# One conversion slot, one load and one buffer offset moved in an attention and feed-forward kernel

## The chip, the cores and the metric

The kernel runs on one core of a Trainium2 chip. Its metric is the device time of one execution in microseconds, and the time of a version is the median of several runs. In the profiles PE is the matrix engine (PEld is its loading of weights), DVE the vector engine, ACT the scalar engine, POOL the general engine, and SP the engine that issues most of the DMAs.

## The reference

```
scores = q @ k.T / sqrt(64) + bias        # 4 batches, 8 heads, 576 x 576; the bias is a small MLP
                                          # of log1p(|i-j|) / log1p(max(i,1)), 8 heads, no batch
attn   = softmax(scores) @ v              # float32
x      = attn, heads side by side         # 2304 tokens x 512
h      = x @ w_in                         # 512 x 2048
out    = (h * tanh(softplus(h))) @ w_out  # 2048 x 512
```

The two weight matrices come in as 64-bit floats, and the kernel itself turns them into 32-bit ones.

## The kernel before

**Three stages.** The bias stage makes the 36 row tiles of the bias, copies each from PSUM to an SBUF tile `bt` (`evac`, lines 500 to 514) and writes it to DRAM. The `bt` tiles take turns in eight buffers. The attention stage follows, and takes over the SBUF memory of the bias stage as soon as the DMAs that read it are done: its tiles `main` and `tail` (lines 266 to 300) lie where `bt` lay. The feed-forward stage comes last. The first three steps of the attention stage run inside the bias stage already.

**A pair and its steps.** The attention stage works on 16 pairs, 0 to 15, each one batch and two heads, in five steps n = 5 i + x of one block of query rows each, in the order 0, 1, 4, 2, 3. The text calls x = 0 to 4 the first to the fifth step. In a step `scores` puts the score matmuls on PE (line 220), `add_bias` lets DVE add the bias and take the row minimum, one instruction for each head (line 237), `exps` lets ACT take the exponentials (line 252), `transposes` turns the tiles of two steps before on PE (lines 287, 290), ACT copies these out of PSUM (lines 295 to 300), and `pv_duo` multiplies with v on PE (lines 313, 317). DVE copies the result out at line 320, which in the fourth step comes behind that step's conversion slots. Block 4 in the third step has half as many rows, so ACT has one exponential there and not two. The scores of a step use both PSUM buffers, so the scores of the next step can't start before `add_bias` has read them.

**Everything is in program order.** Each engine takes its instructions in the order in which the code gives them, so what waits holds back all that is behind it on that engine.

**q and k.** From pair 3 on the scores are three products of a rounded part `hi` and a rest `lo`. `load_qk` of pair i + 1 is called in the first step of pair i: SP loads the raw values into `rawqk` (one buffer, line 166), POOL loads the same values rounded into `qkhi` (two buffers, line 167), and POOL then takes four differences for `qklo` (line 170). Behind the raw load SP has v (line 176) and whatever the step has besides.

**Conversion slots.** `split` spends a number of slots per step on the weights. A job of 512 columns takes four: a multiplication (line 118 on DVE, or line 116 on ACT when its slot falls in the third step), a shift (line 121), and two combining instructions on DVE (lines 123 and 125). Line 123 reads what the multiplication wrote. Line 125 ends the job and issues the load of the next but one (line 104), into the buffer that it has just left. Nine slots fall in a pair, so the phase of the jobs comes round every four pairs. For the first four jobs ACT (line 135) and POOL (line 136) also split the result into two parts.

Of the kernel before, what the change touches and what calls it, by code (L numbers as in the profile page):

```python
# [7 lines left out]
F32 = mybir.dt.float32  # L8
# [7 lines left out]
B, H, S, D, C = 4, 8, 576, 64, 32  # L16
# [3 lines left out]
P = 128  # L20
SH = S // 2
KO = 640
QW = KO + S
# [21 lines left out]
def kernel(ctx: ExitStack, tc, qk, v, wb, w2, w_in, w_out, psia, psi4, rinv, eye, out):  # L45
    nc = tc.nc
    pe, dve, act, pool, sp = nc.tensor, nc.vector, nc.scalar, nc.gpsimd, nc.sync
# [48 lines left out]
    def load_weights():  # L96
        while todo and len(w64) < 2:
            kind, g, k = job = todo.pop(0)
            w = convp.tile([P, 512, 2], U32, name="w64")
            if kind == "i":  # L100
                src = w_in[k * P:(k + 1) * P, g * 512:(g + 1) * 512]
            else:
                src = w_out[(4 * g + k) * P:(4 * g + k + 1) * P, :]
            sp.dma_start(out=w.rearrange("p f t -> p (f t)"), in_=src.bitcast(U32))
            w64.append((job, w))

    def conv_weights(on_act):

        job, w = w64.pop(0)
        late = order.index(job) >= EARLY
        c = (ring if late else convp).tile([P, 512], F32, name="w32")
        cu = c.bitcast(U32)
        if on_act:
            act.mul(c, w.bitcast(F32)[:, :, 1], 2.0 ** -112)
        else:
            dve.tensor_scalar(c, w.bitcast(F32)[:, :, 1], 2.0 ** -112, None, op0=ALU.mult)

        def parts():  # L120
            dve.tensor_scalar(w[:, :, 0], w[:, :, 0], 29, None, op0=ALU.logical_shift_right)
            yield False
            dve.scalar_tensor_tensor(cu, cu, 3, w[:, :, 0], op0=ALU.logical_shift_left, op1=ALU.bitwise_or)  # L123
            yield False
            dve.scalar_tensor_tensor(cu, w[:, :, 1], 0x80000000, cu, op0=ALU.bitwise_and, op1=ALU.bitwise_or)  # L125
            w32.append((job, c))
            yield True
        return parts()

    def split_weights(eng):  # L130
        job, c = w32.pop(0)
        if job not in w_hi:
            w_hi[job] = ring.tile([P, 512], F32R, name="wh{}{}{}".format(*job))
            w_lo[job] = ring.tile([P, 512], F32R, name="wl{}{}{}".format(*job))
        act.copy(w_hi[job], c)
        eng.tensor_tensor(w_lo[job], c, w_hi[job].bitcast(F32), op=ALU.subtract)
# [12 lines left out]
    hip = rsbuf("hip", 2, side="right")  # L149
    biasp = rsbuf("biasp", side="right")  # L150
    s_ps = rpsum("s_ps", 2, side="right")
    qk_t, v_t, bias_t = {}, {}, {}
    PLAIN = 3
    st.tile([P, 32], F32, name="fill", bufs=1)
    x0 = lsbuf("x0")

    def load_qk(i):
        hp, b = divmod(i, B)
        if i < PLAIN:
            qk_t[i] = [rawp.tile([P, 1280], F32, name="qklo")] * 2  # L160
            sp.dma_start(out=qk_t[i][0][:, :QW], in_=qk[b, hp])
            return
        raw = hip.tile([P, 1280], F32, name="rawqk", bufs=1)
        hi = hip.tile([P, 1280], F32R, name="qkhi")
        lo = rawp.tile([P, 1280], F32R, name="qklo")
        sp.dma_start(out=raw[:, :QW], in_=qk[b, hp])
        pool.dma_start(out=hi[:, :QW], in_=qk[b, hp])
        for c0 in (608, 912, 0, 304):
            sl = slice(c0, c0 + 304)
            pool.tensor_tensor(lo[:, sl], raw[:, sl], hi[:, sl].bitcast(F32), op=ALU.subtract)  # L170
        qk_t[i] = hi, lo

    def load_v(i):
        hp, b = divmod(i, B)
        vt = vp.tile([P, 2, 5, D], F32, name="vt")
        sp.dma_start(out=vt, in_=v[b, hp].rearrange("p (h c d) -> p h c d", h=2, c=5))
        v_t[i] = vt

    def load_raw(i):
        load_qk(i)  # L180
        load_v(i)
# [3 lines left out]
    def load_bias(hp, c):  # L185
        h0, h1 = 2 * hp, 2 * hp + 1
        rows = P if c < 4 else 64
        src = bias_d[c][:, :rows * PITCH].rearrange("h (i j) -> h i j", j=PITCH)[:, :, PAD:PAD + S]
        if c < 3 and hp % 2 == 0:
            pool_, name = ((xa, "xhi"), (xa, "xlo"), (x0, "xraw"))[c]  # L190
            t = pool_.tile([P, HP * TB], F32, name=name)[:, :2 * S]
        else:
            t = biasp.tile([P, 2 * S if c < 4 else S], F32, name=f"bias{c}")
        bias_t[hp, c] = t
        if c < 4:
            sp.dma_start(out=t[:, 0:S], in_=src[h0])
            sp.dma_start(out=t[:, S + 64:], in_=src[h1, :, 0:512])
            sp.dma_start(out=t[:, S:S + 64], in_=src[h1, :, 512:S])
        else:
            sp.dma_start(out=t[TOP], in_=src[h0])  # L200
            sp.dma_start(out=t[LOW, 64:], in_=src[h1, :, 0:512])
            sp.dma_start(out=t[LOW, 0:64], in_=src[h1, :, 512:S])

    NPAIR = B * HP
# [129 lines left out]
    def load_x(blk, p):  # L334
        t0, n = blocks[blk]
        raw = p.tile([P, HP, TB], F32, name="xraw", bufs=1)
        for off, m, b, s in _x_runs(t0, n):
            sp.dma_start(out=raw[:, :, off:off + m], in_=x_d[b][:, :, s:s + m])
        x_raw[blk] = raw

    def load_r(blk, r, h0, h1):

        t0, n = blocks[blk]
        for off, m, b, s in _x_runs(t0, n):
            while m:
                k = min(m, 512 - s) if s < 512 else m
                for u in range(2):
                    if s < 512:
                        src = r_d[b][h0:h1, 4 * u:4 * u + 4].rearrange("p c j -> p (c j)")[:, s:s + k]
                    else:  # L350
                        src = r_d[b][h0:h1, 8, 64 * u + s - 512:64 * u + s - 512 + k]
                    sp.dma_start(out=r[64 * u:64 * u + 64, :, off:off + k],
                                 in_=src.unsqueeze(0).to_broadcast([64, h1 - h0, k]))
                off, m, s = off + k, m - k, s + k

    def ahead(n):

        i, x = divmod(n, 5)
        if x == 0 and i + 1 < NPAIR:
            load_raw(i + 1)  # L360
        c = {(1, 3): 0, (2, 1): 1, (2, 3): 2, (3, 2): 4, (3, 4): 3}.get((i % B, x))
        if c is not None and i // B + 1 < HP:
            load_bias(i // B + 1, c)
        if n == NS - 11:
            load_x(0, x0)
        if n == NS - 10:
            x_hi[0] = xa.tile([P, HP, TB], F32R, name="xhi")
            x_lo[0] = xa.tile([P, HP, TB], F32R, name="xlo")
            load_r(0, x_lo[0].bitcast(F32), 0, HP)
        if NS - 5 <= n < NS - 1:  # L370
            d = n - (NS - 5)
            x, hi, lo = (y[0][:, d] for y in (x_raw, x_hi, x_lo))
            dve.tensor_tensor(hi, x, lo.bitcast(F32), op=ALU.mult)
            pool.tensor_tensor(x, x, lo.bitcast(F32), op=ALU.mult)
            pool.tensor_tensor(lo, x, hi.bitcast(F32), op=ALU.subtract)

    def split(n):

        i, x = divmod(n, 5)
        for _ in range(((2, 1, 2, 2, 2) if n > 25 else (2, 1, 3, 2, 2) if n > 4 else (0,) * 5)[x]):  # L380
            if not conv and w64:
                conv.append(conv_weights(x == 2))
            elif conv and next(conv[0]):
                conv.clear()
                load_weights()
                if w32[0][0] in order[:EARLY]:
                    split_weights(pool)
# [55 lines left out]
    bo = bsbuf("bo", 8)  # L443
# [19 lines left out]
    NW = S + 15  # L463

    def reach(t):

        left, right = 16 * t + 15, S - 16 * t
        n = max(left + 1, right)
        return left, right, n + n % 2
# [6 lines left out]
    for idx, t in enumerate(ts):  # L476
        spent["a"] += 1.0 + (1.9 if idx in SOFT_AT else 0.0)
        spent["v"] += (1.7 if idx in SOFT_AT else 0.0)
        n = reach(t)[2]
# [6 lines left out]
    def make_h(idx):  # L486
        if idx >= NB:
            return
        n = reach(ts[idx])[2]
        for cg in range(4):  # L490
            e = maker[idx, cg]
            ht = ring.tile([P, 640], F32, name="ht")
            k = 4 * ts[idx] + cg
            if e == "a":
                act.activation(ht[:, :n], at[:, :n], AF.Relu, bias=bb[:, k:k + 1])
            else:
                dve.tensor_scalar(ht[:, :n], at[:, :n], bb[:, k:k + 1], 0.0, op0=ALU.add, op1=ALU.max)
            h_t[idx, cg] = ht

    def evac(idx):  # L500
# [12 lines left out]
        dst = bias_d[c][:, a:a + 16 * (PITCH + 1)].rearrange("h (i j) -> i h j", j=PITCH + 1)  # L513
        sp.dma_start(out=dst[:, :, :NW], in_=bt)

    make_h(0)
    make_h(1)
    sp.dma_start(out=ident, in_=eye)
    for idx in range(NB + 2):
        if idx < NB:  # L520
            t = ts[idx]
            make_h(idx + 2)
            n = reach(t)[2]
# [218 lines left out]
```

## Time and profile before

| | us |
|---|---|
| three runs, median (lowest to highest) | 702.86 (701.67 to 703.18) |
| the profiled execution's own time | 702.7 |
| its span in the trace | 700.9 |
| of the span, attention steps from the first pair on | 66 to 299 |
| of the span, feed-forward stage | 299 to 700 |

The profiled execution's own time is 1.8 us longer than its span, and 0.2 us under the median of the runs. A timeline row gives the start, the duration, the engine, the line of the kernel and the tiles, and in brackets the engine's idle time before it with what ended that. Neighbouring instructions of one line are merged, and a row of such a merge ends in the number of its instructions.

### The profile page before, as it was taken

The numbers are of one execution on the slowest core, as the hardware profiler recorded it, in microseconds if no ns is written. First come the engines' busy times: TensorE is split into PE (matmuls) and PEld (weight loads), VectorE is DVE, ScalarE is ACT, GpSimd is POOL, SyncE is SP. The second block draws the span as 40 slices with busy tenths as digits, with TensorE's granted clock in tenths as the row PEclk, the third lists the DMA queues.
The fourth block names the chain that finished last, engine by engine and source line by source line (L and its number), as shares of the span: only waits on it lengthen the run. The fifth ranks groups of instructions, "written<-read, shape, count | busy, mean of one in ns | idle before, by whom it ended". The sixth has DMA issues, their size and how long they took to land.

```text
span 700.9 us, 13630 instructions
## 1 busy us (share of the span) xinstructions
PE 672.9 (96%) x5156; PEld 511.2 (73%) x5156; DVE 517.3 (74%) x1082; ACT 458.4 (65%) x987; POOL 72.4 (10%) x85
## 2 busy tenths in 40 slices
PE   5878999999999999999999999999999999999997
PEld 2224666776777666668888888889988888888886
DVE  7995898888988878868788566655775567665554
ACT  6895988888899888876675544444554455454443
POOL 0000142322222222710000000000000000000000
PEclk9999999999999999999999999999999999999999
DMA  4997688787778767204000120023005000010001
GB/s 150 318 285 228 195 273 263 216 284 225 245 234 266 241 231 240 55 22 116 1 1 0 66 56 1 1 76 106 1 1 150 1 1 0 1 60 1 1 0 60
DMA packets 46081, 81.88 MB, mean 117 GB/s; under 512 B 14400, under 2 KB 23104, under 8 KB 46016
## 3 DMA queue, kind: packets, MB, share of 16 engines
q1 hardware_dynamic: 43568, 72.70, 32.8%
q0 software_dynamic: 1872, 8.09, 3.9%
q8 instruction: 40, 0.66, 0.4%
q10 hardware_dynamic: 576, 0.22, 0.1%
q14 instruction: 25, 0.20, 0.1%
HBM read 60.60 MB, written 20.40 MB: 116 GB/s over the span
## 4 chain that ended last, share of the span: by engine, by line
PE 71%; ACT 9%; DVE 7%; DMA 3%; issue 2%; DVEq 0%; ACTq 0%
PE h L589 28%; PE y L627 28%; PE o L313 5%; PE s L220 5%; ACT pt L252 5%; DVE pt L237 4%; ACT main L295 3%; PE tp L287 3%; PE tp L290 1%; DMA w<-in_w_in_dram 1%; DMA w<-in_w_out_dram 1%; PE o L317 1%; DVE w L123 1%; DVE x L320 1%; DVE w L125 1%
## 5 line engine op out<-in xcount | busy, mean ns | idle before, releaser
L252 ACT ACTIVATE pt<-pt,m 128x576 f32<-128x576 f32 x144 | 112.2, 780 | 33.5 <-DVE m L237 32.9
L627 PE MATMUL y<-who,ghi 128*128 128x512 f32 x288 | 112.1, 389 | 0.0
L627 PE MATMUL y<-wlo,ghi 128*128 128x512 f32 x288 | 112.1, 389 | 0.0
L627 PE MATMUL y<-who,glo 128*128 128x512 f32 x288 | 112.0, 389 | 0.0
L611 ACT CAST ghi<-e 128x512 fp32r<-128x512 f32 x72 | 44.7, 621 | 93.5 <-DVE e L607 93.5
L237 DVE CUSTOM_DVE_ANT_0 pt<-s,bias 128x576 f32<-128x576 f32 (+1 forms) x112 | 81.3, 753 | 17.8 <-PE s L220 16.6
L594 ACT ACTIVATE e<-h 128x512 f32<-128x512 f32 x72 | 43.0, 597 | 65.9 <-PE h L589 65.7
L595 DVE TENSOR_SCALAR e<-e 128x512 f32<-128x512 f32 x72 | 30.6, 426 | 74.0 <-ACT e L594 74.0
L612 DVE TENSOR_TENSOR glo<-e,ghi 128x512 fp32r<-128x512 f32 x72 | 49.8, 692 | 44.9 <-ACT ghi L611 44.9
L589 PE MATMUL h<-xhi,whi 128*128 128x512 f32 (+1 forms) x320 | 79.1, 369 | 0.0
L589 PE MATMUL h<-xhi,wli 128*128 128x512 f32 (+1 forms) x320 | 78.7, 368 | 0.0
L589 PE MATMUL h<-xlo,whi 128*128 128x512 f32 (+1 forms) x320 | 78.7, 368 | 0.0
L313 PE MATMUL o<-main,vt 128*64 128x320 f32 (+1 forms) x512 | 73.8, 411 | 3.1 <-DVE x L320 3.0
L295 ACT COPY main<-tp 128x512 f32<-128x512 f32 x126 | 66.5, 577 | 2.0 <-DMA bias_d<-bt 1.9
L287 PE MATMUL tp<-ident,pt 64*128 64x64 f32 x1184 | 61.7, 227 | 6.3 <-ACT main L295 4.7
L589 PEld LDWEIGHTS h<-xhi,whi 128*128 128x128 f32 x320 | 57.1, 188 | 11.7 <-issue 0.7
L287 PEld LDWEIGHTS tp<-ident,pt 64*128 64x128 f32 x1184 | 53.5, 139 | 15.2 <-ACT main L295 13.1
L589 PEld LDWEIGHTS h<-xhi,wli 128*128 128x128 f32 x320 | 56.9, 189 | 10.0
L589 PEld LDWEIGHTS h<-xlo,whi 128*128 128x128 f32 x320 | 56.9, 189 | 10.0
L627 PEld LDWEIGHTS y<-who,glo 128*128 128x128 f32 x288 | 54.1, 188 | 11.3
L627 PEld LDWEIGHTS y<-who,ghi 128*128 128x128 f32 x288 | 54.1, 188 | 11.0
L627 PEld LDWEIGHTS y<-wlo,ghi 128*128 128x128 f32 x288 | 54.1, 188 | 10.9
(69 smaller groups left out, 1126.9 us busy)
## 6 DMA issues: line engine op xcount, KB each, us to landing
bias_d<-bt SPq DMA_DIRECT2D x36, 295.5 KB
w<-in_w_in_dram SPq DMA_DIRECT2D x16, 512.0 KB
w<-in_w_out_dram SPq DMA_DIRECT2D x16, 512.0 KB
qkhi<-in_qk_dram POOLq DMA_DIRECT2D x13, 608.0 KB, 4.5
rawqk<-in_qk_dram SPq DMA_DIRECT2D x13, 608.0 KB
vt<-in_v_dram SPq DMA_DIRECT2D x16, 320.0 KB
out_dram<-w SPq DMA_DIRECT2D x17, 256.0 KB
x_d<-x SPq DMA_DIRECT2D x32, 128.0 KB
```

What stands on the lines that cost most here:

```text
L220: pe.matmul(s[:, j, :SH], q[rows, c * P:(c + 1) * P], k[rows, KO + j * SH:KO + (j + 1) * SH], start=(t == 0), stop=(t == len(terms) - 1))
L237: dve.tensor_tensor_reduce(out=halves(pt[rows, sl]), in0=s[rows, :, :SH], in1=halves(bt[rows, sl]), scale=-0.125, scalar=BIG, op0=ALU.add, ...
L252: act.activation(ps, ps, AF.Exp, bias=m[:, u:u + 1], scale=-1.0, accum_out=sums[i][:, k:k + 1])
L287: pe.transpose(tp[:, k * 64:k * 64 + 64], pt[rows, c0:c0 + P], ident[rows, rows])
L295: copy(main[:, :, :, q0:q0 + 64], tp.rearrange("p (h k q) -> p h k q", h=2, k=4))
L313: pe.matmul(o[h * 64:h * 64 + 64, :w], vt[:, h, k, :], main[:, h, k, :], start=(k == 0), stop=False, **kw)
L589: pe.matmul(h[:, u * n:(u + 1) * n], w["i", g4, d][:, r * P:(r + 1) * P], x[:, d, :n], start=(k == 0), stop=(k == 11))
L594: act.activation(e, h, AF.Exp)
L595: dve.tensor_scalar(e, e, E20, None, op0=ALU.min)
L611: act.copy(ghi, e)
L612: dve.tensor_tensor(glo, e, ghi.bitcast(F32), op=ALU.subtract)
L627: pe.matmul(ys[blk][t], g[:, c0:c0 + P], w, start=(f == 0 and k == 0), stop=(f == NFC - 1 and k == 2))
```

## The change

Three things are moved. The conversion slots per step go from (2, 1, 2, 2, 2) to (2, 1, 3, 1, 2) after step 25, and from (2, 1, 3, 2, 2) to (2, 2, 3, 1, 2) in steps 5 to 25. The raw load of a pair is issued in the fourth step of the pair but one before it, two steps sooner than it was; the rounded load and the differences on POOL stay where they were in the code. And four `bt` tiles that nothing uses are taken ahead of the bias stage's first one, so that each row tile uses the buffer that is four further on in the turn.

```diff
+    def load_plain(i):
+        hp, b = divmod(i, B)
+        qk_raw[i] = hip.tile([P, 1280], F32, name="rawqk", bufs=1)
+        sp.dma_start(out=qk_raw[i][:, :QW], in_=qk[b, hp])
...
-        raw = hip.tile([P, 1280], F32, name="rawqk", bufs=1)
+        raw = qk_raw.pop(i)
         hi = hip.tile([P, 1280], F32R, name="qkhi")
         lo = rawp.tile([P, 1280], F32R, name="qklo")
-        sp.dma_start(out=raw[:, :QW], in_=qk[b, hp])
         pool.dma_start(out=hi[:, :QW], in_=qk[b, hp])
...
         if x == 0 and i + 1 < NPAIR:
             load_raw(i + 1)
+        if x == 3 and PLAIN <= i + 2 < NPAIR:
+            load_plain(i + 2)
...
-        for _ in range(((2, 1, 2, 2, 2) if n > 25 else (2, 1, 3, 2, 2) if n > 4 else (0,) * 5)[x]):
+        for _ in range(((2, 1, 3, 1, 2) if n > 25 else (2, 2, 3, 1, 2) if n > 4 else (0,) * 5)[x]):
...
+    for _ in range(4):
+        bo.tile([P, NW], F32, name="bt")
     make_h(0)
     make_h(1)
```

## Rows read from the trace of the kernel before

**Rows 1.** The page, busy time, share of the span and instructions of each engine.
```profile
PE 672.9 (96%) x5156; PEld 511.2 (73%) x5156; DVE 517.3 (74%) x1082; ACT 458.4 (65%) x987; POOL 72.4 (10%) x85
```

**Rows 2.** Windows over the attention steps: busy us (instructions) by engine, PE clock, DMA.
```profile
66.00:299.00 233.00, 226.04 (x2816) 160.81 (x2813) 199.29 (x499) 200.44 (x523) 68.89 (x77) 1.00 0.71 226
```

**Rows 3.** Timeline of pair 10, third to fifth step: start us, us, engine, line.
```profile
215.33 0.70 ACT L116 ACTIVATE w<-w 128x512 f32<-128x512 f32 x1
...
215.72 0.76 DVE L237 CUSTOM_DVE_ANT_0 pt<-s,xraw 128x576 f32<-128x576 f32 x1 [1.84 <-PE s L220]
...
217.09 0.71 DVE L123 SCALAR_TENSOR_TENSOR w<-w,w 128x512 uint32<-128x512 uint32 x1
...
217.83 0.69 DVE L125 SCALAR_TENSOR_TENSOR w<-w,w 128x512 uint32<-128x512 uint32 x1
...
218.32 0.29 PE L220 MATMUL s<-qkhi,qklo 64*128 64x288 f32 x2
...
218.44 0.48 DVE L320 COPY x<-o 128x320 f32<-128x320 f32 x1
...
218.84 0.75 DVE L237 CUSTOM_DVE_ANT_0 pt<-s,bias 128x576 f32<-128x576 f32 x1
...
219.69 0.78 ACT L252 ACTIVATE pt<-pt,m 128x576 f32<-128x576 f32 x1 [0.35 <-DVE m L237]
```

**Rows 4.** Timeline of pair 12, second to fifth step.
```profile
241.29 0.36 SPq L166 DMA_DIRECT2D rawqk<-in_qk_dram  x1
...
242.22 0.38 SPq L104 DMA_DIRECT2D w<-in_w_out_dram  x1
...
245.41 3.22 POOL L170 TENSOR_TENSOR qklo<-rawqk,qkhi 128x304 fp32r<-128x304 f32 x4 [10.37 <-DMA rawqk<-in_qk_dram]
...
248.53 0.30 PE L220 MATMUL s<-qkhi,qklo 64*128 64x288 f32 x2
...
248.74 0.43 DVE L118 TENSOR_SCALAR w<-w 128x512 f32<-128x512 f32 x1 [1.36 <-DMA w<-in_w_out_dram]
...
249.82 0.74 DVE L237 CUSTOM_DVE_ANT_0 pt<-s,bias 128x576 f32<-128x576 f32 x1
```

**Rows 5.** Timeline, fourth to fifth step, first and last of 13 pairs (2, 14).
```profile
94.91 1.24 PE L220 MATMUL s<-qklo 64*128 64x288 f32 x8
...
97.05 0.74 DVE L237 CUSTOM_DVE_ANT_0 pt<-s,bias 128x576 f32<-128x576 f32 x1
...
279.50 0.30 PE L220 MATMUL s<-qkhi,qklo 64*128 64x288 f32 x2
...
280.01 0.75 DVE L237 CUSTOM_DVE_ANT_0 pt<-s,bias 128x576 f32<-128x576 f32 x1
```

**Rows 6.** Timeline, conversion instructions that run while POOL subtracts.
```profile
122.88 0.71 DVE L123 SCALAR_TENSOR_TENSOR w<-w,w 128x512 uint32<-128x512 uint32 x1
...
187.06 1.11 DVE L118 TENSOR_SCALAR w<-w 128x512 f32<-128x512 f32 x1
...
229.07 1.27 DVE L123 SCALAR_TENSOR_TENSOR w<-w,w 128x512 uint32<-128x512 uint32 x1
```

**Rows 7.** The page's DMA issues: KB each, median us to landing.
```profile
qkhi<-in_qk_dram POOLq DMA_DIRECT2D x13, 608.0 KB, 4.5
```

**Rows 8.** Timeline of POOL, pairs 9 and 10.
```profile
204.09 0.57 POOL L167 DMA_DIRECT2D qkhi<-in_qk_dram  x1 [1.66 <-PE tp L287]
...
213.86 1.62 POOL L170 TENSOR_TENSOR qklo<-rawqk,qkhi 128x304 fp32r<-128x304 f32 x2 [9.21 <-DMA rawqk<-in_qk_dram]
```

**Rows 9.** Timeline, first step of pair 15.
```profile
282.86 0.76 DVE L237 CUSTOM_DVE_ANT_0 pt<-s,bias 128x576 f32<-128x576 f32 x1 [1.41 <-PE s L220]
```

**Rows 10.** Timeline, end of the bias stage.
```profile
58.41 0.59 ACT L295 COPY main<-tp 128x512 f32<-128x512 f32 x1 [1.91 <-DMA bias_d<-bt]
...
60.84 0.33 SPq L196 DMA_DIRECT2D bias<-bias_d  x1
...
64.10 0.76 DVE L237 CUSTOM_DVE_ANT_0 pt<-s,bias 128x576 f32<-128x576 f32 x1 [2.98 <-PE s L220]
```

More of the change, by code (lines that the diff above doesn't have):

```diff
@@ L151 @@
     s_ps = rpsum("s_ps", 2, side="right")
-    qk_t, v_t, bias_t = {}, {}, {}
+    qk_raw, qk_t, v_t, bias_t = {}, {}, {}, {}
     PLAIN = 3
```

## The prediction

> **What bounds the kernel now.** I read the page first. PE is busy for 672.9 us of the 700.9 us span [rows 1], so time is won only where PE stands still or runs slowly. Then the windows by stage: over the attention steps PE is busy for 226.0 of 233.0 us, DVE for 199.3 and ACT for 200.4 [rows 2]. Each of the three has some slack, and all three are bound to one another in every step. No instruction of the feed-forward stage is moved, so I look only at these 233 us and at the handoff ahead of them.
>
> Then the timeline of one pair, to see who waits for whom. In pair 10 the fourth step's bias addition starts at 215.72, and DVE has waited 1.84 us for PE's scores: up to here PE sets the time. From there DVE doesn't stop. It runs two additions, the conversion instructions of lines 123 and 125, and the copy of line 320, and comes to the fifth step's addition at 218.84. The scores for it were done at 218.32 + 0.29 = 218.61, so the addition is 0.23 us late. ACT then starts the fifth step's exponential at 219.69, after 0.35 us of waiting for it [rows 3]. The third step thus has spare DVE time, and the fourth has none.
>
> The same lateness stands in the 13 pairs from 2 to 14. In the first of them it is 97.05 - 96.15 = 0.90 us, in the last 280.01 - 279.80 = 0.21 us, and the 13 together make 6.0 us [rows 5]. It is largest where something holds DVE up. In pair 12 DVE waits 1.36 us for a load of weights that was issued at 242.22, behind the raw q and k at 241.29, and the addition comes at 249.82 for scores that were done at 248.83, 0.99 us late [rows 4].
>
> **The slot that leaves the fourth step.** It takes one conversion instruction of 0.43 to 0.71 us out of a step in which DVE is late, and puts it into the 1.84 us for which DVE waits in the third [rows 3, 4]. Without it, and with the weights there in time, the fifth step's addition can follow its scores at once. Four pairs I leave out here (3, 6, 10 and 14; next part). The other nine hold 4.4 of the 6.0 us. Some 0.03 us in each stays for the handover from PE, and I take 0.1 off for pairs 8 and 12 (below): **-4.0 us**. If the cover in the third step were gone, the addition of the fourth step would be late by what the slot lasts; and next in line after DVE is PE, which has no spare time in these steps. So the gain lies between 0 and -6.0 us.
>
> **The wait that comes with it.** A job's multiplication runs on ACT when its slot falls in the third step, and line 123 of that job reads its result. In pair 10 the third step's slots are a multiplication on ACT and the shift on DVE, and line 123 comes behind the fourth step's additions, at 217.09. The change puts it ahead of them. But ACT's multiplication starts at 215.33 only, behind its copies, and ends at 216.03. So line 123 can't start before that, ends at 216.74, and the addition that now starts at 215.72 is queued behind it: 1.02 us late [rows 3]. The scores of the next step, ACT's exponential and all that follows them wait with it. ACT had 0.35 us of waiting before the fifth step's exponential, which absorbs a part: 1.02 - 0.35 = 0.7 us. DVE alone would lose less: 216.74, two additions at their present spacing (217.09 - 215.72 = 1.37), 0.69 for line 125 and 0.48 for the copy give 219.3 against 218.84, or 0.4 us. Nine slots per pair and four per job bring this phase back in pairs 6, 10 and 14. With the pattern of steps 5 to 25 it comes in pairs 1 and 3, and there the second step has one slot more as well, which delays the multiplication further: I take 0.9 us for these two. 3 x 0.7 + 2 x 0.9 = **+3.9 us**, between 5 x 0.4 = 2.0 and 5 x 1.3 = 6.5 (with the whole of a 0.7 us slot on top in the early pairs, and as much for a collision in the others).
>
> **ACT as a new reader of the weights.** In pairs 8 and 12 the moved slot is the multiplication itself, which goes to ACT and is wanted at about 0.4 us before the fourth step's addition, at 245.5 in pair 12. Raw, v and w, 1440 KB, took 248.74 - 241.29 = 7.45 us; after raw had landed at 245.41 the other 832 KB took 3.3 us, or 250 KB per us [rows 4]. Without raw's 608 KB w should land some 2.4 us sooner, at about 246.2 (an estimate from these rows). ACT is then held up by 0.7 us, and most of it lies in the time in which it waits for the addition anyway. That is the 0.1 us above.
>
> **The raw load, two steps sooner.** POOL's four differences wait for raw now: in pair 10 they begin at 213.86. The rounded load is issued at 204.09 [rows 8], and such a load takes 4.5 us [rows 7], so with raw there they can begin at 208.6, some 5.3 us earlier. SP issues the same DMAs as before, in another order. Raw (0.36 us to issue [rows 4]) now goes ahead of the fourth step's bias loads and result writes, and v and w of the next first step move up. There is one raw buffer, so the load waits for the differences of the pair before; these take 3.2 us from 208.6 on and end in the second step, and SP doesn't stop. If they ended later, SP would stand with the result writes, v and the weights behind it. The loads themselves save nothing but what is in the sums above, and in the last pair: its first addition waited 1.41 us for scores [rows 9], part of them for differences whose raw load was late. I take **-0.4 us** of it, between 0 and -1.4.
>
> The differences now run beside other DVE work, though. Beside them a conversion instruction of 0.43 or 0.71 us took 1.11 and 1.27 us, but another one kept its 0.71 [rows 3, 4, 6]: a delay of 0 to 0.7 us. Till now it fell on the third and fourth steps, and is part of the lateness above. In future it falls on the end of the first step and on the second. The second step's delay goes into the third step's 1.84 us, of which the moved slot leaves 1.1 us. It is not covered where line 123 waits for ACT, in five pairs: I take 0.2 us for each, **+1.0 us**, between 0 and one full delay in each of 13 pairs, 9 us.
>
> The Trainium skill, SBUF — State Buffer, section "Who interferes with whom", makes this a lock: a DVE instruction with two SBUF inputs or in a two-port mode and a POOL instruction that reads SBUF exclude each other, and whichever starts later is fully blocked. The three rows agree with it, delays of 0.7, 0.6 and none; by the rule alone each pair could lose the rest of one difference, which is the second rival below.
>
> **The row tiles' buffers.** The first `main` copy waits 1.91 us for a write out of a `bt` tile and starts at 58.41. The last row tile has landed by 60.84, when SP can issue the load that needs it [rows 10]. Turning the buffers by four gives `main` other predecessors. If they are all early ones, the copy starts up to 1.9 us sooner. But the fifth step's addition at 64.10 needs the bias loaded from 60.84 on, which doesn't move. I take **-0.6 us**, between -1.2 and, if a late row tile comes to lie under `main`, 60.84 - 58.41 = +2.4.
>
> **The sum.** -4.0 + 3.9 + 1.0 - 0.4 - 0.6 = -0.1 us. The profiled execution's own time was 702.7 us, so the changed kernel should take **702.6 us**, against a median of 702.86. About 0.2% (1.4 us) is what a measurement of this kernel can tell from no change.
>
> **The rivals.**
> 1. *Faster: the new wait costs only what DVE loses.* ACT's copies might be done sooner, since the additions ahead of them are. Then the five pairs lose 0.4 us each, and 3.9 becomes 2.0: 700.7 us. For it speaks that DVE and PE have nothing else to wait for there; against it that ACT's multiplication stands behind a whole step of its own. Together with the full -1.2 at the handoff it is 700.1.
> 2. *Slower: the differences block the first step.* When the rounded load lands at 208.6, the first step's last slot may just be ahead. If POOL is first in each of the 13 pairs, DVE loses 0.3 us more on average (half of 0.6), and ACT's exponentials behind it have no slack there: +3.9 us, less the 1.0 already counted, 705.5 us. It decides from about 0.2 us per pair. The lock of the page named above would work in this way.
> 3. *Slower: the handoff.* A late row tile under `main` or `tail` stops ACT until 60.84: 2.4 us instead of -0.6, so 705.6 us.
> 4. *The early raw load does nothing*, because the rounded load lands late when both are in flight: then the differences stay in the third step, in which the slots are now. The w loads still gain. Some +1 us, within the forecast's own range of 701.3 to 704.0.
>
> **Chances.** The forecast, with rival 4, has 0.37: the sum of gains and the sum of new waits are alike in size. Rival 1 has 0.36, since the gains are read off directly as waits, and the losses are bounded more loosely. Rival 2 has 0.16, and rival 3 has 0.11. So faster 0.36, same 0.37, slower 0.27. The range runs from 700.0 to 705.2 us: it leaves out about one in ten below, where the new wait costs next to nothing, and one in ten above.
>
> **What would show it.** In the fourth step of pairs 2, 7 and 12 no wait for weights, and the fifth step's addition right behind its scores. In pairs 1, 3, 6, 10 and 14 line 123 in the third step starting when line 116 ends, and a late addition behind it; if DVE doesn't wait there, my second term is wrong. POOL's differences should start about 4.5 us after line 167. The first `main` copy shows the handoff: at about 57 us, 58.4 or 60.8.

## The result and the profile after

The changed kernel takes 706.25 us (median of 19 runs, 702.96 to 709.17) against 702.07 us of 19 runs of the kernel before on the same chips. The ratio is 1.0051, with a 95% interval of 1.0035 to 1.0067: slower by 2.5 to 4.7 us, where 702.6 us and no change were forecast. The profiled execution took 706.25 us, its span is 704.2 us.

The page's row of busy times now reads, against [rows 1],

```profile
PE 676.4 (96%) x5156; PEld 511.3 (73%) x5156; DVE 519.3 (74%) x1078; ACT 460.1 (65%) x991; POOL 74.1 (11%) x85
```

The first question is where these microseconds arise. One stretch holds all the steps that the change touches: from the first bias addition of pair 1 to that of the fifth step of pair 15. I call it the stretch; it can be read off any trace, and what happens at the handoff ahead of it doesn't enter. Here it is in the kernel before, by the view of windows (us, busy us and instructions of PE, PEld, DVE, ACT, POOL, then PE's clock, DMA share and GB/s):

```profile
67.92:295.74 227.82, 220.86 (x2782) 157.28 (x2778) 197.43 (x495) 197.42 (x514) 66.74 (x76) 1.00 0.72 228
```

And in the changed kernel:

```profile
67.18:299.03 231.85, 224.14 (x2782) 157.61 (x2778) 199.38 (x490) 199.05 (x518) 68.61 (x76) 1.00 0.68 224
```

231.85 - 227.82 = 4.03 us are lost in the attention steps; the rest of the span behind them takes 405.2 us in both kernels. PE's idle time grows by 0.75 us only, from 227.82 - 220.86 = 6.96 to 231.85 - 224.14 = 7.71. The other 3.3 us stand in its busy time, though it runs the same 2782 matmuls at the same clock. So PE's busy time, with which my prediction began, hides most of this loss. The Trainium skill, Perfetto Trace Analysis, says in its opening remark that matmul busy time is a bad measure of how close a kernel comes to its limit, because matmuls are pipelined. The trace agrees in so far as the busy time of the same 2782 matmuls differs by 3.28 us.

The view of DVE's waits names new ones (engine and line, what it waited for, us in all, times, longest). Changed kernel, over the stretch:

```profile
DVE pt L241 <- PE s L224: 16.7, 23, 1.4
DVE w L123 <- ACT w L116: 9.1, 5, 2.2
DVE x L324 <- PE o L321: 2.0, 6, 0.8
...
DVE w L121 <- DMA w<-in_w_out_dram: 0.4, 1, 0.4
```

Kernel before:

```profile
DVE pt L237 <- PE s L220: 22.9, 32, 1.9
DVE w L121 <- DMA w<-in_w_out_dram: 1.8, 1, 1.8
...
DVE w L118 <- DMA w<-in_w_out_dram: 1.7, 2, 1.4
...
DVE w L118 <- DMA w<-in_w_in_dram: 0.7, 1, 0.7
```

DVE waits 6.2 us less for scores, and the waits for weights are nearly gone, but it waits 9.1 us in five places for ACT's multiplication, and 2.0 us for PE at line 324. (Lines below 160 are the same in both kernels, later ones stand four lower.) The timeline shows one of the five, the third step of pair 10, against [rows 3]:

```profile
215.26 0.43 DVE L121 TENSOR_SCALAR w<-w 128x512 uint32<-128x512 uint32 x1
...
217.14 0.70 ACT L116 ACTIVATE w<-w 128x512 f32<-128x512 f32 x1
217.21 0.30 PE L224 MATMUL s<-qkhi,qklo 64*128 64x288 f32 x2
217.87 0.69 DVE L123 SCALAR_TENSOR_TENSOR w<-w,w 128x512 uint32<-128x512 uint32 x1 [2.18 <-ACT w L116]
218.59 0.76 DVE L241 CUSTOM_DVE_ANT_0 pt<-s,xraw 128x576 f32<-128x576 f32 x1
```

The scores were done at 217.21 + 0.30 = 217.51. The addition that wants them comes at 218.59, 1.08 us late, behind a line 123 that could not start before ACT was done at 217.84.

What was won shows in pair 12, against [rows 4]. The weights are issued sooner, with no raw load ahead of them, and ACT's multiplication finds them there:

```profile
243.17 0.38 SPq L104 DMA_DIRECT2D w<-in_w_out_dram  x1
...
248.07 0.70 ACT L116 ACTIVATE w<-w 128x512 f32<-128x512 f32 x1
...
248.51 0.76 DVE L241 CUSTOM_DVE_ANT_0 pt<-s,bias 128x576 f32<-128x576 f32 x1 [0.90 <-PE s L224]
```

DVE waits for scores there, and for nothing else up to the fifth step: the fourth lasts 3.05 us instead of 3.89.

The second loss is in the first step of pair 13, where POOL's differences now run:

```profile
252.00 0.57 POOL L171 DMA_DIRECT2D qkhi<-in_qk_dram  x1 [6.43 <-PE tp L291]
...
254.25 0.75 DVE L241 CUSTOM_DVE_ANT_0 pt<-s,bias 128x576 f32<-128x576 f32 x1
...
256.10 3.57 POOL L174 TENSOR_TENSOR qklo<-rawqk,qkhi 128x304 fp32r<-128x304 f32 x4 [3.53 <-DMA qkhi<-in_qk_dram]
256.19 1.02 DVE L118 TENSOR_SCALAR w<-w 128x512 f32<-128x512 f32 x1
257.14 1.05 DVE L121 TENSOR_SCALAR w<-w 128x512 uint32<-128x512 uint32 x1
258.11 0.74 DVE L241 CUSTOM_DVE_ANT_0 pt<-s,bias 128x576 f32<-128x576 f32 x1
```

The differences start 4.10 us after their load was issued and 1.85 us after the step's first addition. In the kernel before the step's two slots read

```profile
254.44 0.39 DVE L118 TENSOR_SCALAR w<-w 128x512 f32<-128x512 f32 x1
254.74 0.42 DVE L121 TENSOR_SCALAR w<-w 128x512 uint32<-128x512 uint32 x1
```

Now they take 1.02 and 1.05 us, and the step lasts 258.11 - 254.25 = 3.86 us instead of 2.62.

Pair by pair, the time from one pair's first addition to the next pair's, read from the timelines (us; the other columns are experiments, below):

| pair | before | changed | early load alone | slots alone | changed, no differences | changed, no differences, multiplication on DVE |
|---|---|---|---|---|---|---|
| 1 | 15.30 | 15.73 | 15.30 | 15.81 | 15.74 | 15.53 |
| 2 | 16.50 | 16.30 | 16.41 | 16.16 | 16.41 | 15.97 |
| 3 | 15.37 | 16.38 | 14.68 | 15.87 | 15.87 | 14.97 |
| 4 | 15.54 | 16.37 | 15.44 | 18.49 | 15.43 | 15.44 |
| 5 | 14.67 | 15.51 | 14.51 | 15.37 | 14.80 | 14.51 |
| 6 | 15.02 | 15.78 | 15.00 | 15.91 | 15.76 | 15.06 |
| 7 | 16.07 | 15.31 | 15.30 | 15.33 | 15.29 | 15.31 |
| 8 | 15.11 | 15.03 | 15.05 | 15.02 | 15.04 | 15.05 |
| 9 | 14.79 | 14.52 | 14.50 | 14.52 | 14.52 | 14.51 |
| 10 | 15.01 | 15.79 | 15.01 | 15.80 | 15.79 | 15.06 |
| 11 | 15.32 | 15.30 | 15.31 | 15.48 | 15.28 | 15.31 |
| 12 | 15.88 | 15.05 | 15.04 | 15.04 | 15.04 | 15.05 |
| 13 | 14.95 | 15.72 | 15.09 | 14.59 | 14.51 | 14.51 |
| 14 | 15.41 | 16.17 | 15.19 | 15.78 | 15.78 | 15.06 |
| stretch | 227.82 | 231.85 | 224.72 | 232.05 | 228.14 | 224.22 |

Pairs 2, 7, 8, 9 and 12 are shorter in the changed kernel, as forecast. Pairs 1, 3, 6, 10 and 14, which wait for ACT, are longer, and so are 4, 5 and 13.

Each column is one execution, and some of it is luck: where a step has to wait for weights differs from execution to execution. With raw loaded late, DVE's waits for weights in fourth steps stand in pairs 2, 7 and 12 in the kernel before (0.36, 0.66 and 1.36 us), but in pair 8 alone (1.73) in the kernel with only the turn of the tiles, whose stretch is as long. So a single pair can be 1 us off by chance, and the sums should be read together with the medians of the runs.

### The profile page after: what moved, and what is told of

Read it like the earlier page. It is cut to its first block, busy times and chain, and to the rows that moved or that the text cites. A ratio compares the mean times of both kernels' runs of the same rounds, so it can differ in the third digit from the quotient of the medians.

```text
span 704.2 us, 13648 instructions
## 1 busy us (share of the span) xinstructions
PE 676.4 (96%) x5156; PEld 511.3 (73%) x5156; DVE 519.3 (74%) x1078; ACT 460.1 (65%) x991; POOL 74.1 (11%) x85
## 4 chain that ended last, share of the span: by engine, by line
PE 69%; ACT 10%; DVE 9%; issue 3%; DMA 2%; SPq 0%; ACTq 0%; DVEq 0%
PE h L597 28%; PE y L635 28%; DVE pt L241 5%; ACT pt L256 5%; PE s L224 4%; PE o L317 4%; ACT main L299 4%; PE tp L291 3%; DVE w L123 1%; PE tp L294 1%; PE o L321 1%; DMA bias<-bias_d 1%; DVE w L125 1%; DMA bias_d<-bt 1%; ACT main L303 0%
## 5 line engine op out<-in xcount | busy, mean ns | idle before, releaser
L291 PE MATMUL tp<-ident,pt 64*128 64x64 f32 x1184 | 63.4, 227 | 7.0 <-ACT main L299 5.4
```

The source lines that it names most:

```text
L291: pe.transpose(tp[:, k * 64:k * 64 + 64], pt[rows, c0:c0 + P], ident[rows, rows])
```

## The experiments

Two theories stood against each other. A: the loss is the wait of line 123 for ACT. B: it comes from POOL's differences, which the earlier load of raw q and k has moved into the first two steps. After the first four runs A was widened to both, and in the expectations of the later runs B or the rival is what each of them is set against. Each ratio is to the kernel before, timed on the same chip, with its 95% interval; "stretch" is that of the profiled execution.

**The parts, each alone, on the kernel before.** The first run has only the hunk of `split`, the second only those of `load_plain`, `load_qk` and `ahead`, the third only that of the dummy tiles.

Slots alone:

```
-        for _ in range(((2, 1, 2, 2, 2) if n > 25 else (2, 1, 3, 2, 2) if n > 4 else (0,) * 5)[x]):
+        for _ in range(((2, 1, 3, 1, 2) if n > 25 else (2, 2, 3, 1, 2) if n > 4 else (0,) * 5)[x]):
```

> Only the new slot pattern, on the kernel before. Theory A (the loss is the wait of line 123 for ACT's multiplication): pairs 1, 3, 6, 10 and 14 are each 0.4 to 1.0 us longer, +3.7 us together as in the changed kernel, and the other pairs win 1.5 to 2 us in the fourth step, less than in the changed kernel, because the loads of weights stay behind raw q and k: about +2 us, ratio 1.003. Theory B (the loss comes from POOL's differences, which run in the first two steps when raw is early): without the early load nothing is lost, -0.5 to -2 us, ratio 0.997 to 0.999.

Measured: ratio 1.0065 (1.0041 to 1.0089), stretch +4.2 us against the kernel before. The five pairs lose 3.1 us together (the 0.4 to 0.9 us of theory A), pairs 2, 7, 8, 9, 12 and 13 win 2.6 us, and pairs 4 and 5 lose 3.7 us more. That last part was in neither theory. In pair 4 of this one execution the timeline has

```profile
125.93 0.43 DVE L121 TENSOR_SCALAR w<-w 128x512 uint32<-128x512 uint32 x1 [1.58 <-DMA w<-in_w_out_dram]
125.93 0.69 ACT L116 ACTIVATE w<-w 128x512 f32<-128x512 f32 x1 [3.42 <-DMA w<-in_w_out_dram]
```

These weights were issued at 118.95, right behind raw at 118.01, and came 7.0 us later. With raw still loaded late, ahead of the weights, the job that now begins sooner finds its weights missing, on DVE and on ACT.

Earlier load alone:

```
+        if x == 3 and PLAIN <= i + 2 < NPAIR:
+            load_plain(i + 2)
...
-        raw = hip.tile([P, 1280], F32, name="rawqk", bufs=1)
+        raw = qk_raw.pop(i)
...
-        sp.dma_start(out=raw[:, :QW], in_=qk[b, hp])
```

> Only the earlier load of raw q and k, on the kernel before. Theory A: the waits for weights in pairs 2, 7 and 12 go (-1.5 us), and the collisions of POOL with DVE in the first two steps cost about as much: -1 to +1 us, ratio 0.999 to 1.001. Theory B: the collisions of the first and second step alone make +3 us or more, ratio 1.004.

Measured: ratio 0.997 (0.9946 to 0.9994), stretch -3.1 us. That is better than theory A's 0.999 to 1.001, though the interval just reaches it, and theory B's 1.004 is refuted. Here the fourth step still has two slots. In pair 9 it reads

```profile
196.66 0.76 DVE L241 CUSTOM_DVE_ANT_0 pt<-s,xraw 128x576 f32<-128x576 f32 x1 [1.54 <-PE s L224]
...
198.02 0.44 DVE L121 TENSOR_SCALAR w<-w 128x512 uint32<-128x512 uint32 x1
...
198.56 0.69 DVE L123 SCALAR_TENSOR_TENSOR w<-w,w 128x512 uint32<-128x512 uint32 x1
...
199.17 0.48 DVE L324 COPY x<-o 128x320 f32<-128x320 f32 x1
...
199.25 0.29 PE L224 MATMUL s<-qkhi,qklo 64*128 64x288 f32 x2
...
199.58 0.76 DVE L241 CUSTOM_DVE_ANT_0 pt<-s,bias 128x576 f32<-128x576 f32 x1
```

The addition follows the scores (199.25 + 0.29 = 199.54) by 0.04 us with two slots in the step: it lasts 2.92 us, as in the changed kernel with one slot. In the kernel before it lasted 3.22, because its line 121 took 0.74 us beside a difference.

Turn of the tiles alone:

```
+    for _ in range(4):
+        bo.tile([P, NW], F32, name="bt")
```

> Only the row tiles' buffers turned by four, on the kernel before. Both theories: the first main copy starts some 0.8 us sooner and pair 1 begins 0.7 us sooner; nothing else moves: -0.7 us, ratio 0.999. If the place of the tiles matters elsewhere too, another number.

Measured: ratio 0.9993 (0.9969 to 1.0017), stretch 227.79. The first `main` copy reads, against [rows 10],

```profile
58.52 0.58 ACT L295 COPY main<-tp 128x512 f32<-128x512 f32 x1 [1.97 <-DMA bias_d<-bt]
```

It waits as long as before. In the changed kernel this copy started at 57.63, but so it did in two kernels without the turn (57.33 with the earlier load alone, 57.45 with the slots alone). Over all 16 profiled executions the first addition of pair 1 lies between 65.37 and 68.80; the eight with the turn have a mean of 67.7, the eight without it 67.2. The turn moves nothing that shows; what differs there differs from one execution to the next. A gain of 0.6 us lies within the interval, though, and the medians can't exclude it.

**The multiplication on DVE.** The changed kernel, with ACT taken out of those third steps in which its product is read at once.

```
-        for _ in range(((2, 1, 3, 1, 2) if n > 25 else (2, 2, 3, 1, 2) if n > 4 else (0,) * 5)[x]):
+        for k in range(((2, 1, 3, 1, 2) if n > 25 else (2, 2, 3, 1, 2) if n > 4 else (0,) * 5)[x]):
...
-                conv.append(conv_weights(x == 2))
+                conv.append(conv_weights(x == 2 and k > 0))
```

> The changed kernel, but a job's multiplication stays on DVE where it would be the first slot of a third step, so that line 123 of the same step no longer waits for ACT. Theory A: DVE works 0.45 us more in the third step of pairs 1, 3, 6, 10 and 14 and fits into its former wait for PE; their loss of 3.7 us goes, but for the collisions: about 703 us, ratio 1.000 (0.998 to 1.001). Theory B: the loss of these pairs only changes its place, 705.5 to 706.5 us, ratio 1.005.

Measured: 702.67 us against 702.48, ratio 0.9992 (0.9968 to 1.0016), stretch 226.27. That is 5.6 us less than in the changed kernel: 2.7 in the five pairs, 2.6 in pairs 4, 5 and 13, where the differences began 0.5 to 1.1 us later in this execution and met fewer slots, and 0.3 in pair 2. The wait for ACT is gone and hasn't come back elsewhere, so theory A holds for it. Pair 10's third step now has three conversion instructions on DVE, and DVE still waits for PE:

```profile
211.51 0.43 DVE L118 TENSOR_SCALAR w<-w 128x512 f32<-128x512 f32 x1
...
211.86 0.44 DVE L121 TENSOR_SCALAR w<-w 128x512 uint32<-128x512 uint32 x1
...
212.33 0.69 DVE L123 SCALAR_TENSOR_TENSOR w<-w,w 128x512 uint32<-128x512 uint32 x1
...
213.42 0.76 DVE L241 CUSTOM_DVE_ANT_0 pt<-s,xraw 128x576 f32<-128x576 f32 x1 [0.39 <-PE s L224]
```

**The differences left out.** These two kernels and the third below leave POOL's four subtractions out; all loads and matmuls stay.

```
         hi = hip.tile([P, 1280], F32R, name="qkhi")
-        lo = rawp.tile([P, 1280], F32R, name="qklo")
         pool.dma_start(out=hi[:, :QW], in_=qk[b, hp])
-        for c0 in (608, 912, 0, 304):
-            sl = slice(c0, c0 + 304)
-            pool.tensor_tensor(lo[:, sl], raw[:, sl], hi[:, sl].bitcast(F32), op=ALU.subtract)
-        qk_t[i] = hi, lo
+        qk_t[i] = hi, hi
```

On the changed kernel:

> The changed kernel without POOL's differences: they are left out, and the products take the rounded q and k in place of the small parts (the same matmuls, the same loads). Theory A, as the first four runs have left it (two losses: line 123's wait for ACT, and POOL's differences beside the slots that stand in the first and second step): the 0.6 to 1.2 us that the second step of pairs 2, 3 and 4 and the first step of pairs 5, 13 and 14 last longer go, about -3.5 us against the changed kernel, ratio to before 1.000; line 123 still waits about 2 us in pairs 3, 6, 10 and 14. Theory B (all is the wait for ACT): no more than -1 us, ratio 1.004.

Measured: ratio 0.9999 (0.9982 to 1.0015), stretch -3.7 us against the changed kernel, from pairs 3 (0.5), 4 (0.9), 5 (0.7), 13 (1.2) and 14 (0.4). The two slots of pair 13's first step are back:

```profile
255.51 0.38 DVE L118 TENSOR_SCALAR w<-w 128x512 f32<-128x512 f32 x1
255.81 0.42 DVE L121 TENSOR_SCALAR w<-w 128x512 uint32<-128x512 uint32 x1
```

The five waits for ACT stay.

On the kernel before:

> The kernel before with the same differences left out. Theory A: the lateness of its fourth steps came from the differences beside two slots and from late weights, not from the number of slots: with two slots still there the fourth step comes down to 2.9 to 3.1 us wherever the weights are there (pairs 3, 5, 8, 9, 13), and only the waits for weights in pairs 2, 7 and 12 stay: -2 us, ratio 0.997. Theory B (two slots are too many for a fourth step): they stay at 3.1 us and over, -0.5 us at most, ratio 0.9995.

Measured: ratio 0.9961 (0.9938 to 0.9984), stretch -3.6 us. With two slots, the fourth step of pairs 5, 9 and 13 lasts 2.93 us (3.08, 3.22 and 3.37 before), that of pair 8 3.02 us. So two slots fit there; what made DVE late was the differences, and weights that came late. Not all of the 3.6 us is the differences': DVE's waits for weights stand in pairs 4 and 7 in this execution (1.30 and 0.57 us) and no longer in 2 and 12, and these four pairs together are 1.4 us shorter.

**Both losses away.** The changed kernel with the two edits above together.

> The changed kernel without POOL's differences (left out, the rounded q and k stand in for the small parts) and with a job's multiplication on DVE where it would be the first slot of a third step: both losses of theory A are taken away at once. Theory A: it comes to where the kernel before came without its differences, ratio to before 0.995 to 0.997, and pairs 6, 10 and 14 last 15.0 to 15.3 us instead of 15.8. So the moved slot wins nothing of its own. Rival (the moved slot does win in the fourth step, and the two losses hide it): 2 us or more below that kernel, ratio 0.993 or less.

Measured: ratio 0.9952 (0.9933 to 0.9972), stretch 224.22, the same as that of the kernel before without its differences. Pairs 6, 10 and 14 last 15.06 us each. The equal sums are partly chance: here pairs 1 to 3 are 0.7 us longer and pairs 4 and 7, without waits for weights, 1.1 us shorter. But the fourth steps of pairs 5, 8, 9, 12 and 13 agree within 0.03 us with two slots and with one, and the rival's 0.993 lies just outside the interval. So the rival is refuted: once nothing delays the fourth step, the moved slot wins nothing, or at most the 0.08 us that pairs 6, 10 and 14 show.

**Old pattern in the early steps.** The changed kernel with

```
-        for _ in range(((2, 1, 3, 1, 2) if n > 25 else (2, 2, 3, 1, 2) if n > 4 else (0,) * 5)[x]):
+        for _ in range(((2, 1, 3, 1, 2) if n > 25 else (2, 1, 3, 2, 2) if n > 4 else (0,) * 5)[x]):
```

> The changed kernel with the old pattern in steps 5 to 25, so that the second step of the early pairs has one slot again and pairs 1 and 3 don't wait for ACT. Theory A: pairs 1 to 5 give back what they lose against the earlier load alone, 0.4 + 1.7 + 0.9 + up to 1.0 us: -3 us against the changed kernel, ratio to before 1.001. Theory B (the wait for ACT alone): only pairs 1 and 3 give something back, -1.2 us, ratio 1.0035.

Measured: 703.11 against 702.37 us, ratio 1.0004 (0.9983 to 1.0025), as theory A said. Pairs 1 to 5 together are 4.0 us shorter than in the changed kernel: 0.4, 0, 1.7, 0.9 and 1.0.

This edit together with the multiplication on DVE leaves only the late part of the moved slot:

> The changed kernel with the old pattern in steps 5 to 25 and with a job's multiplication on DVE where it would be the first slot of a third step. It differs from the earlier load alone (ratio 0.997) by the place of the moved slot from step 26 on and by the turn of the tiles. Theory A: the fourth step is at what PE's scores allow with one slot as with two, 2.9 to 3.1 us; so pairs 7, 8, 9, 11 and 12 last as long as there, and the sum is the same within 1 us: ratio 0.996 to 0.998. Rival (the slot wins in the fourth step): 2 us below that, 0.994.

Measured: ratio 0.998 (0.9963 to 0.9997). Pairs 7, 8, 11 and 12 last as long as with the earlier load alone, within 0.02 us, and the rival's 0.994 lies outside the interval. In pair 9 the differences caught the first step in this execution (15.09 us), and in pair 14 DVE waited 2.78 us for the last weights.

**When the rounded load and the raw load are issued.** On the earlier load alone, first with the rounded load and the differences one step later in the code,

```
         if x == 0 and i + 1 < NPAIR:
-            load_raw(i + 1)
+            if i + 1 < PLAIN:
+                load_qk(i + 1)
+            load_v(i + 1)
+        if x == 1 and PLAIN <= i + 1 < NPAIR:
+            load_qk(i + 1)
```

> The earlier load of raw q and k alone (old slots, no turn of the tiles), with the rounded load and POOL's differences issued one step later. Theory A: the differences then fall on the end of the second step and on the third, where DVE waits for scores; the collisions that the earlier load alone still has (the third step of pair 2, the first of pair 13) go: -0.5 to -1.5 us against that kernel, ratio to before 0.995. Theory B: they only move on to the third step's slots and come late again in the fourth: +0.5 to +1.5 us against it, ratio 0.999.

Measured: ratio 0.9994 (0.9972 to 1.0017); theory A's gain didn't come. But from pair 4 on the rounded load is issued no later than without the edit, within 0.1 us. The one that pair 13 calls for, with the addition of pair 12's fifth step ahead of it, reads with the earlier load alone

```profile
244.71 0.76 DVE L241 CUSTOM_DVE_ANT_0 pt<-s,bias 128x576 f32<-128x576 f32 x1 [0.49 <-PE s L224]
245.15 0.57 POOL L171 DMA_DIRECT2D qkhi<-in_qk_dram  x1 [5.71 <-PE tp L291]
```

and in this kernel

```profile
248.17 0.76 DVE L241 CUSTOM_DVE_ANT_0 pt<-s,bias 128x576 f32<-128x576 f32 x1 [0.49 <-PE s L224]
248.60 0.57 POOL L171 DMA_DIRECT2D qkhi<-in_qk_dram  x1 [5.37 <-PE tp L291]
```

In both POOL is idle for over 5 us, waits for PE, and issues the load 0.44 and 0.43 us after that addition's start. There are two `qkhi` buffers, and from the third load on POOL has to wait for one to come free, whatever step the code names. So this run says nothing of a load that is really issued later. It is longer than the earlier load alone in pairs 2 and 3, where the load did move (1.6 us; pair 3 waits 2.14 us for weights in its third step), and in pairs 13 and 14, whose first steps collide (3.87 and 3.62 us). Whether the late issue causes the wait for weights was not tested further.

Then with the raw load in the fifth step (`x == 4` for `x == 3` in `ahead`):

> The earlier load of raw q and k alone, but issued in the fifth step of the pair ahead instead of the fourth, so one step sooner than in the kernel before and not two. Theory A (what it wins comes from the differences leaving the fourth step and from the weights going ahead): raw still lands before the rounded load does, and before the weights are asked for: the same as the earlier load alone, ratio 0.996 to 0.998. Rival (the weights need the whole lead): the waits for weights in pairs 2, 7 and 12 come back, +1.5 us, 0.999 or more.

Measured: ratio 0.9978 (0.9953 to 1.0003), stretch 224.22. One step of lead does what two do in this execution: of the waits for weights in pairs 2, 7 and 12 only 0.31 us in pair 12 is left. By the ratio alone the rival's 0.999 isn't excluded.

**Smaller differences.** The changed kernel with

```
-        for c0 in (608, 912, 0, 304):
-            sl = slice(c0, c0 + 304)
+        for c0 in (608, 760, 912, 1064, 0, 152, 304, 456):
+            sl = slice(c0, c0 + 152)
```

> The changed kernel with each of POOL's four differences cut in two (eight of 152 columns). Theory A with a lock: an instruction of DVE that meets a difference waits until that one ends, so the worst delay is halved, to some 0.3 us from 0.63; but more of DVE's instructions meet one: the first steps of pairs 5, 13 and 14 are 0.3 to 0.6 us shorter, -1 us in all, ratio 1.004. Rival (the two share the port in turns, and a delay depends only on how long POOL works): the same delays or longer ones, ratio 1.005 to 1.007.

Measured: ratio 1.0023 (1.0 to 1.0046), stretch -2.7 us against the changed kernel: more than expected. Some of that is luck again: in pair 5 (-0.7) the differences began 3.29 us after the first addition and met no slot of the first step. Pair 13's first step reads

```profile
254.14 1.43 POOL L174 TENSOR_TENSOR qklo<-rawqk,qkhi 128x152 fp32r<-128x152 f32 x2 [3.60 <-DMA qkhi<-in_qk_dram]
254.16 0.39 DVE L118 TENSOR_SCALAR w<-w 128x512 f32<-128x512 f32 x1
...
254.46 0.74 DVE L121 TENSOR_SCALAR w<-w 128x512 uint32<-128x512 uint32 x1
```

Line 121 takes 0.74 us where it took 1.05 beside the larger differences and 0.42 without any: the delay is 0.32 instead of 0.63 us. Over all kept traces the longest delay of a conversion instruction beside a difference is 0.69 us with the larger ones and 0.41 with the smaller, and a difference by itself lasts 0.83 and 0.50 us: the delay shrinks as POOL's instruction does, as a lock would have it, and unlike the rival.

**The version that beats both.** The earlier load alone, with the differences in eight, first with the raw load in the fourth step, then in the fifth:

> The earlier load of raw q and k alone (old slots, no turn of the tiles), with POOL's four differences cut into eight. Theory A with the lock: what that kernel still loses to the differences (0.6 us in the first step of pair 13, 1.0 in pair 2) is halved: -0.5 to -1 us against it, ratio to before 0.996. Rival: the four more instructions on POOL make the differences end later, and more of DVE's instructions meet one: the same or slower, 0.997 to 0.999.

> The same with the raw load in the fifth step. Theory A: the same within what can be measured, ratio 0.995 to 0.9975. Rival: 0.998 to 1.000.

Measured: 698.98 us against 702.57, ratio 0.9947 (0.9927 to 0.9967), and 700.26 us, ratio 0.9962 (0.9947 to 0.9977). The first has the lowest ratio of the complete kernels of this study, but its lead over the earlier load alone (0.997) is inside the intervals, so what the eight add isn't shown. Its stretch is 224.07, against 224.72 there; pair 13's first step lasts 2.90 us, with line 121 at 0.74. The second's profiled execution took 705.63 us, out of line with its median: in pair 14 DVE waited 5.20 us for the last weights (last section).

## Why the prediction was wrong

The time came out 1 us above the upper end of the range. The steps, one by one, in us of the stretch:

**The step that failed** is the last paragraph but one of "The raw load, two steps sooner": the delays of DVE beside POOL's differences, put at +1.0 us between 0 and 9. They cost **+3.7 us** (231.85 with them, 228.14 without; by the medians 0.52% of 702 us, 3.7 us). The mechanism was right, its size wasn't. The text placed the delays at the end of the first step and in the second, and took it that the third step's waiting covers them except in five pairs. But in pairs 5, 13 and 14 the differences caught a slot of the first step, which has no cover: 3.67, 3.86 and 3.50 us instead of 2.62, 2.62 and 2.98. And in pairs 3 and 4 the second step had been given a second slot, and lasted 3.56 and 3.69 us where it lasts 3.03 and 2.46 without the differences, more than the third step could give back. The first step is the place that the second rival named; it came in three pairs instead of thirteen. What decides is when the rounded load lands. In the changed kernel differences that began 1.65, 1.85 and 2.04 us after the first addition collided; in pair 9, at 2.31 us, they didn't. The seven profiled kernels with an early raw load and four differences agree: in pairs 5, 9 and 13 all nine that began by 2.21 us lengthened the first step to 3.22 us or more, and all twelve from 2.28 us on left it at 2.61 to 2.64. The prediction had 2.3 us for pair 10, from a median load time, on the edge of this, and took one value for all pairs.

By the Trainium skill, SBUF — State Buffer, section "Who interferes with whom", a DVE instruction in a two-port mode, or with two SBUF inputs against a POOL instruction that reads SBUF, shares a port pair with POOL under an exclusive lock, and the later of the two is fully blocked. The traces agree: with POOL's instruction cut from 0.83 to 0.50 us the longest delay fell from 0.69 to 0.41 us.

**"The slot that leaves the fourth step": -4.0.** A gain of about this size came: 227.82 - 224.22 = 3.6 us of the stretch, if both losses are taken away, and 3.2 us in the nine fourth steps that were meant. But it doesn't belong to the slot. The earlier load alone brings 3.1 us of it, the kernel before without its differences 3.6, and with the slot moved as well it is 224.22 again. The lateness of [rows 5] was read rightly as DVE being late, and wrongly as too many slots: the instructions in those steps had been stretched by a collision or held up by weights. The slot alone does win 2.6 us in six pairs while raw is loaded late; the two edits remove the same lateness, once.

**"The wait that comes with it": +3.9.** Right in place, and nearly in size. Line 123 waits in pairs 1, 3, 6, 10 and 14 and in no other. 228.14 - 224.22 = 3.9 us go when the multiplication moves to DVE (both without differences), 3.3 of them in the five pairs and 0.7 in pairs 2 and 5, which the prediction didn't name; that the sum is 3.9 to the tenth is luck. In pairs 6, 10 and 14 it is 0.70, 0.73 and 0.72 us, against the 0.7 worked out; the 0.9 for the two early pairs was 0.2 and 0.9. The first rival, a wait that costs only 0.4 us each, is refuted: four of the five pairs lost 0.7 us or more.

**"ACT as a new reader of the weights."** In pair 12 of the changed kernel the weights issued at 243.17 are there when ACT's multiplication starts at 248.07, no more than 4.9 us later, against 6.5 us behind raw [rows 4]. No wait shows in pairs 7, 8 and 12. Right.

**The rest of "The raw load".** For the last pair -0.4 stood, and nothing was won: DVE waits 1.39 us for scores before its first addition, against 1.41, and the step ahead of it lasts 2.83 us against 2.84. Raw is not the cause now, since the differences end 9.9 us ahead of that addition. Pair 14 is one of the five whose third step waits for ACT, and the fifth step lasts 2.84 us in pairs 3, 6 and 10 of the changed kernel too; with the earlier load alone it is 2.46 in pair 14, 0.4 less, as was forecast. That this is raw's doing isn't shown, since with the turn of the tiles alone it is 2.46 as well. The differences start 3.9 to 5.8 us after their load's issue from pair 5 on (4.5 was forecast), so the fourth rival, an early raw load that does nothing, falls.

**"The row tiles' buffers": -0.6.** Nothing that shows, in the kernel with the turn alone; the term lies outside the stretch. The third rival, a late tile under `main`, didn't come either: the copy started at 57.63, in the span of what single executions show.

The sum by what was measured is -3.6 + 3.9 + 3.7 = +4.0 us. It meets the stretch's own difference by construction, since each term is the difference of two stretches in a row of four kernels. The medians of the runs, each set against the kernel before on its own chip, bear it out: -3.4, +3.3 and +3.7 us, each known to within 2 us.

## What to carry to other kernels

An engine that is late in a step need not have too much work in it: see first whether its instructions last longer there than elsewhere, and what runs beside them. If so, move the neighbour and leave the work. When work is moved earlier, look up where its new time falls in each period and not in the mean one: a transfer whose landing varies by 1 us decides from pair to pair whether it meets a step without slack, and a load that waits for a buffer is issued when that comes free and not where the code has it. And an instruction moved ahead of a wait takes its producers along: where the product comes from another engine, move that too, or give it to the engine that waits.

## What was not expected of the hardware

The last load of weights, in the same place of all kernels, took very different times. In the changed kernel it was issued at 270.39 and waited for until 277.90, 7.5 us; in the kernel before 8.6 us (267.76 to 276.34), with the earlier load alone 8.9 us (262.71 to 271.64). In the slowest case the timeline has

```profile
265.77 1.25 SPq L104 DMA_DIRECT2D w<-in_w_out_dram  x1
...
277.32 0.43 DVE L121 TENSOR_SCALAR w<-w 128x512 uint32<-128x512 uint32 x1 [5.20 <-DMA w<-in_w_out_dram]
```

11.6 us, beside the loads of x and of the reciprocals that start in these steps; it made pair 14 last 19.99 us instead of 15.2. Why it takes longer in one execution than in another stays open; no run here was made for it.
